# Third group's queries and keys as 32 by 32 tiles, its masks and exponentials inside the first output product, state sums of 40 columns behind the first group

## The chip, the cores and the metric

One of the eight cores of a Trainium2 chip runs the kernel. Its engines work side by side: TensorE (PE) multiplies matrices into PSUM, VectorE (DVE), ScalarE (ACT) and GpSimd (POOL) work on tiles, and the SP queue issues most DMAs. The metric is the time of one execution on the device in microseconds, the median of several.

## The reference

Two blocks follow each other. The first is an mLSTM cell on 4 batches of 8 heads (32 batch-heads), 768 steps, head dimension 40. Each step updates a state of 40 by 40 and a vector of 40 per head, with exponential gates that are kept stable by a running maximum m:

```python
m_new = np.maximum(f_gate[:, :, t] + m, i_gate[:, :, t])
f_stab = np.exp(f_gate[:, :, t] + m - m_new)
i_stab = np.exp(i_gate[:, :, t] - m_new)
C = f_stab[:, :, None, None] * C + i_stab[:, :, None, None] * np.einsum('bhd,bhe->bhde', vt, kt)
n = f_stab[:, :, None] * n + i_stab[:, :, None] * kt
h_tilde = np.einsum('bhde,bhe->bhd', C, qt)
denom = np.maximum(np.abs(nq), 1.0)          # nq = n . q
y[:, :, t] = o * h_tilde / denom             # o = sigmoid(o_gate)
```

The second takes the result as 3072 tokens of 320 features through a SwiGLU block with 1536 hidden features: `(silu(x @ w_gate) * (x @ w_val)) @ w_out`. The activations are float32; the three weight matrices arrive as float64 and are converted on the chip.

## The kernel before, in words

The 768 steps are cut into six groups of 128 steps (n = 0 to 5), each of two halves of 64. For a group, the cell works in a chunked form. Scores are the products of keys and queries (`scores`, L327). Weights come from the gates: `weights_load` fetches the running maxima to `w_sb`, `weights_sub` (L441) subtracts, `weights_mask` (L446) sets what lies in the future to a very small number on GpSimd, `weights_exp` (L450) takes exponentials on ScalarE. `weigh` (L334) multiplies scores by weights. `weigh_values` (L337) makes the weighted values `vw_sb`, `add` (L348) sums keys times weighted values for the state, and `next_state` decays the state on GpSimd (L357) and adds the sum on VectorE (L359). `attend` makes the parts from the state (L367) and from within the half (L372), `gather`, `gate` and `divide` finish the cell's output. Heads come in pairs, and pairs in two parts, P = 0 and 1.

`scores` and `attend` need keys and queries with features on partitions (`kT`, `qT`). There are two ways to get there. `turn` transposes on TensorE: loads of whole rows go to `k_sb` and `q_sb`, 32 transposes for each P (L292) go to PSUM, and eight copies (L117, L119) for the two P bring them to SBUF. `turn_squares` (L317) lets VectorE transpose blocks of 32 by 32 in SBUF, and wants its input loaded as such blocks: `load_squares` (L311) issues 16 small DMAs for each tensor, into a tile of zeros, as 40 features leave 24 of 64 rows empty. Groups 1 and 2 use `turn`, groups 3 to 5 use `turn_squares`. `q_sq` is a view of `q_sb`; the tile `k_sq` is allocated after the first output product, with a memset (L748). `k_sb` keeps plain keys for `add`.

The second block of group g runs beside the cell of group n = g + 1. `hidden(g, m)`, for twelve blocks m, multiplies by gate and value weights (L634, 20 products into two PSUM banks), ScalarE applies Silu (L639) and VectorE the product (L640). The output product of group 0 is `project_all` (L657): four banks, one per batch, summed over m in step. Later groups use `project` (L650), a batch at a time. `result` copies a bank to `z_sb` (two buffers, L644) and sends it. PSUM has two rings of four banks, "gen" for L634, L650 and L657, and "cell" for the attention. In group 0 the weights are converted as well: `convert` scales on ScalarE (L186, L188), joins on VectorE (L195, L196) and rounds on GpSimd or VectorE (L203).

Nothing is planned by a scheduler. The order of each engine's instructions is the order in which the program writes them; semaphores then hold each until its inputs are there. `slots` (L706 for group 0, L754 for later ones) and `after` (L725) list what is written behind block m of `hidden` and of `project_all`. Behind `project_all` before the change stand, in this order, the four output copies (in `result`), the third group's two exponentials, its two sigmoids (`sig`, L453) and its weighted values (L737 to L742). The transposes of group 2 are in slots 0 and 1 of g = 1.

Of the kernel before, what the change touches and what calls it, by code (L numbers as in the profile page):

```python
# [9 lines left out]
F32 = mybir.dt.float32  # L10
# [4 lines left out]
ALU = mybir.AluOpType  # L15
# [3 lines left out]
L = 128  # L19
SUB = 64  # L20
# [4 lines left out]
def kernel(  # L25
# [18 lines left out]
    nc = tc.nc  # L44
    B, H, S, D = q.shape
# [4 lines left out]
    PP = BH // 2  # L50
    DP = 64
# [5 lines left out]
    NKC = DM // HP  # L57
# [13 lines left out]
    conv = early_scope.enter_context(tc.tile_pool(name="conv", bufs=2))  # L71
# [4 lines left out]
    def bank(name, tag="cell"):  # L76
        return psum.tile([128, 512], F32, name=name, tag=tag)

    def half(i):
        return slice(i * SUB, (i + 1) * SUB)  # L80

    def heads(P):
        return slice(P * UH, (P + 1) * UH)

    k_sb = const.tile([128, BH, DP], F32)
    q_sb = const.tile([128, BH, DP], F32)
    v_sb = const.tile([128, BH, D1], F32)
    o_sb = const.tile([128, BH, D], F32)
    w_sb = const.tile([128, BH, SUB], F32)
    vw_sb = const.tile([128, BH, D1], F32)  # L90
    kT = const.tile([128, PP, L], F32)
    qT = const.tile([128, PP, L], F32)
# [150 lines left out]
    for u in range(B):  # L243
        r = slice(u * BH, (u + 1) * BH)
# [58 lines left out]
    SQ = 32  # L303

    def load_squares(dst, a, c):
        for two in range(2):
            for s in range(2):
                r = slice((2 * two + s) * SQ, (2 * two + s + 1) * SQ)
                w = min(SQ, D - s * SQ)
                for t in range(L // SQ):  # L310
                    nc.sync.dma_start(out=dst[r, :, t, 0:w],  # L311
                                      in_=a[:, two:H:2, ds(c * L + t * SQ, SQ), ds(s * SQ, w)].rearrange("b h p d -> p (b h) d"))

    def turn_squares(src, dst):
        for P in range(2):
            a = slice(P * UA, (P + 1) * UA)
            nc.vector.transpose(out=dst[:, a].rearrange("p a t -> p (a t)"), in_=src[:, a].rearrange("p a t d -> p (a t d)"))  # L317

    q_sq = q_sb.rearrange("p (a x) d -> p a (x d)", x=2).rearrange("p a (t d) -> p a t d", d=SQ)
# [16 lines left out]
    def weigh_values(eng, P):  # L336
        eng.tensor_tensor(vw_sb[:, heads(P)], v_sb[:, heads(P)], w_sb[:, heads(P), last].to_broadcast([128, UH, D1]),  # L337
                          op=ALU.mult)

    def small(name, n=UA):  # L340
        return bank(name)[:, 0:n * D1].rearrange("p (a d) -> p a d", d=D1)

    def add(P):
        ps = [small("add") for _ in range(2)]
        for a in range(UA):
            for i, two in QUAD:
                h = P * UH + 2 * a + two
                nc.tensor.matmul(ps[i][half(two), a, :], lhsT=k_sb[half(i), h, :], rhs=vw_sb[half(i), h, :],  # L348
                                 start=True, stop=True)
        return ps  # L350

    def state(s):
        return C_ring[s % 3]

    def next_state(s, P, ps):
        a = slice(P * UA, (P + 1) * UA)
        nc.gpsimd.tensor_tensor(state(s + 1)[:, a], state(s)[:, a],  # L357
                                dec[:, s - 2, a].unsqueeze(2).to_broadcast([128, UA, D1]), op=ALU.mult)
        nc.vector.tensor_tensor(state(s + 1)[:, a], state(s + 1)[:, a], ps, op=ALU.add)  # L359


    def attend(n, P):
# [86 lines left out]
    def weights_exp(P):  # L449
        nc.scalar.activation(w_sb[:, heads(P)], w_sb[:, heads(P)], AF.Exp)  # L450

    def sig(P):
        nc.scalar.activation(o_sb[:, heads(P)], o_sb[:, heads(P)], AF.Sigmoid)  # L453
# [7 lines left out]
    def rows(u):  # L461
        return slice(u * BH, (u + 1) * BH)

    A, V, G = nc.scalar, nc.vector, nc.gpsimd
# [188 lines left out]
    def project_all(g, after):  # L653
        ps = [bank("o_ps", "gen")[:, 0:DM] for _ in range(B)]
        for m in range(NFC):
            for u in range(B):
                nc.tensor.matmul(ps[u], lhsT=hid(g, m)[:, ts(u, L)], rhs=wo_sb[:, m, :], start=(m == 0),  # L657
                                 stop=(m == NFC - 1))
            for f in after.get(m, ()):
                f()  # L660
        for u in range(B):
            result(g, u, ps[u])

    live = {}
# [5 lines left out]
    def do_weigh(P):  # L670
        weigh(P, live.pop(("sp", P)))

    def do_add():
        for P in range(2):
            live["add", P] = add(P)

    def do_state(s, P):
        for i, ps in enumerate(live.pop(("add", P))):
# [16 lines left out]
    def load_all(dst, a, n):  # L695
# [3 lines left out]
    run = lambda f, *a: (lambda: f(*a))  # L699
# [6 lines left out]
    slots = {  # L706
        0: [run(first_state, 1, A), run(load_all, k_sb, k, 1), run(load_all, q_sb, q, 1)],
        1: [run(late_maxima), run(piece_load, 6, h_sb[:, NH - NKC:])],
        2: [run(weights_load, 1), run(load_all, v_sb, v, 1), run(decay_rows)],
        3: [run(late_turns)],  # L710
        4: [run(decay)],
        5: [run(turn, 0, (A, A), (A, V))],
        6: [run(turn, 1, (A, A), (A, V)), run(piece_load, 7)],
        7: [run(weights_sub, 1, 0), run(weights_sub, 1, 1), run(weights_mask, 0), run(weights_mask, 1)],
        8: [run(weights_exp, 0), run(weights_exp, 1), run(weigh_values, G, 0), run(weigh_values, G, 1),
            run(piece_load, 8)],
        9: [run(do_scores), run(do_weigh, 0), run(do_weigh, 1), run(load_all, o_sb, o_gate, 1)],
        10: [run(do_add), run(do_state, 2, 0), run(do_state, 2, 1)],
        11: [run(do_attend, 1, 0), run(do_gather, 1, 0, False), run(piece_load, 9)],
    }  # L720
    for m in range(NFC):
        hidden(0, m, [run(convert, j, V if j in on_vector else None) for j in ahead[m]])
        for f in slots.get(m, ()):
            f()
    after = {  # L725
        0: [run(do_attend, 1, 1), run(convert, 14), run(sig, 0), run(sig, 1), run(do_gate, 0)],
        1: [run(do_gather, 1, 1), run(weights_load, 2), run(load_all, v_sb, v, 2)],
        2: [run(do_divide, 1, 0), run(convert, 15)],
        3: [run(do_divide, 1, 1), run(load_all, k_sb, k, 2), run(load_all, q_sb, q, 2), run(load_all, o_sb, o_gate, 2)],
        4: [run(convert, 16), run(seam, 1, 0, (A, V, A, V))],  # L730
        5: [run(seam, 1, 1, (A, V, A, V))],
        6: [run(convert, 17)],
        8: [run(weights_sub, 2, 0), run(weights_mask, 0)],
        9: [run(weights_sub, 2, 1), run(weights_mask, 1)],
    }
    project_all(0, after)
    weights_exp(0)  # L737
    weights_exp(1)
    sig(0)
    sig(1)  # L740
    weigh_values(G, 0)
    weigh_values(G, 1)  # L742
    early_scope.close()
    late = ctx.enter_context(tc.tile_pool(name="late", bufs=1))
    xTs.append(late.tile([128, NKC, TW], F32, name="xT1"))
# [1 line left out]
    k_sq = late.tile([128, PP, L // SQ, SQ], F32, name="k_sq")  # L747
# [4 lines left out]
    for g in range(1, NG):  # L752
        n, f = g + 1, g + 2
        slots = {m: [] for m in range(NFC)}  # L754
        if n < NG:
            slots[0] = [run(turn, 0, (A, V), (A, V))] if n == 2 else [run(turn_squares, q_sq, qT)]
            slots[1] = [run(turn, 1, (A, V), (A, V))] if n == 2 else [run(turn_squares, k_sq, kT)]
            if n == 2:
                slots[1].append(run(nc.gpsimd.memset, q_sb, 0.0))
            slots[3] = [run(do_scores), run(do_weigh, 0)]  # L760
            slots[4] = [run(do_weigh, 1)]
            slots[5] = [run(do_add), run(do_state, 2 * n, 0)]
            slots[6] = [run(do_state, 2 * n, 1)]
            slots[7] = [run(do_attend, n, 0), run(do_gather, n, 0)]
            slots[8] = [run(do_divide, n, 0), run(send_squares, 0)]
            slots[9] = [run(do_attend, n, 1), run(do_gather, n, 1)]
            slots[10] = [run(do_divide, n, 1), run(send_squares, 1)]
        if f < NG:
            slots[2] += [run(load_squares, q_sq, q, f), run(load_squares, k_sq, k, f)]
            slots[5].append(run(load_all, k_sb, k, f))  # L770
            slots[9] += [run(load_all, v_sb, v, f), run(weights_load, f)]
            slots[10].append(run(load_all, o_sb, o_gate, f))
        for m in range(NFC):
            hidden(g, m)
            for s in slots[m]:
                s()
        for u in range(B):
            if f < NG and u < 2:
                weights_sub(f, u)
                weights_mask(u)  # L780
            if f < NG and u == 2:
                weights_exp(0)
                weights_exp(1)
                sig(0)
                sig(1)
                weigh_values(nc.gpsimd, 0)
                weigh_values(nc.gpsimd, 1)
            if n < NG and u >= 2:
                turn_inputs(n, 2 * u - 4)
                turn_inputs(n, 2 * u - 3)  # L790
            project(g, u)
# [30 lines left out]
```

## Time and profile before

| | before |
|---|---|
| median of 3 runs | 568.58 us (565.74 to 569.22) |
| profiled execution | 567.32 us, its span 565.2 us |
| TensorE busy | 554.4 us, 98% |
| weight loads / VectorE / ScalarE / GpSimd busy | 57% / 40% / 25% / 18% |
| mean granted TensorE clock | 0.996 |
| DMA | 45.05 MB, mean 80 GB/s |

Times in the trace count from the span's start. Up to about 55 us the kernel loads its inputs and does the first group's attention; `hidden` of group 0 lasts to about 100 us, `project_all` to about 133 us, and each later group takes some 87 us. A row of the timeline has a start, a length, the engine, the line, the operation, its output and input tiles, and in brackets the idle time of the engine before it with what ended that. In the chain of work that ended last, a row has a start, a length, the engine and the line.

### The profile page before, as it was taken

Reading aid. Unit: us, or ns where it says so; the run is one execution under the profiler, and the core shown is the slowest. Engines: PE = TensorE matmul, PEld = TensorE weight load, DVE = VectorE, ACT = ScalarE, POOL = GpSimd, SP = SyncE. Lnnn points to the kernel's source line nnn. Section 1 sums busy time; section 2 is a strip of 40 time slices with the busy share of each in tenths; the row PEclk is TensorE's granted clock in tenths of the full one; section 3 lists DMA queues with packets and bytes.
Section 4 is the critical chain, followed back from the end, with each engine's and each line's share of the span. In section 5 each row is a group of like instructions: output and inputs, shape, how many; then the busy total and the mean of one; then the engine's idle time right before and its main releaser. Section 6 shows DMA issues by size and latency. Waiting matters only on the chain.

```text
span 565.2 us, 11653 instructions
## 1 busy us (share of the span) xinstructions
PE 554.4 (98%) x5055; PEld 322.7 (57%) x5056; DVE 225.4 (40%) x379; ACT 139.3 (25%) x208; POOL 103.8 (18%) x95
## 2 busy tenths in 40 slices
PE   8997999999999999999999999999999999999997
PEld 4855545665555476455566455567455557544475
DVE  5775576880334531434612424613432631011100
ACT  4365446435401015110104201104211010111100
POOL 2132344555211123002105001206001100000000
PEclk9999999999999999999999999999999999999999
DMA  9999991594362395353295253196000131000000
GB/s 124 182 271 187 179 264 22 151 152 95 41 79 26 50 148 110 44 53 49 38 149 111 41 66 49 31 145 110 24 2 2 26 59 46 12 1 1 1 23 24
DMA packets 211227, 45.05 MB, mean 80 GB/s; under 512 B 201736, under 2 KB 206344, under 8 KB 211176
## 3 DMA queue, kind: packets, MB, share of 16 engines
q1 hardware_dynamic: 208596, 40.14, 44.5%
q10 hardware_dynamic: 2580, 4.16, 3.3%
q8 instruction: 40, 0.66, 0.5%
q14 instruction: 11, 0.09, 0.1%
HBM read 35.03 MB, written 4.01 MB: 69 GB/s over the span
## 4 chain that ended last, share of the span: by engine, by line
PE 84%; DMA 5%; SPq 4%; DVE 3%; ACT 2%; POOL 1%; issue 1%; ACTq 0%; DVEq 0%; POOLq 0%
PE gv_ps L634 49%; PE o_ps L650 23%; PE o_ps L657 5%; SPq L113 3%; DMA raw<-in_moe_w_val_dram 3%; DMA h_sb<-in_moe_w_gate_dram 2%; PE intra L372 2%; PE inter L367 2%; PE sp L327 1%; PE add L348 1%; DVE wgv_sb L196 1%; DVE wgv_sb L195 1%; POOL C L357 1%; PE tp_kq L292 0%; SPq L161 0%
## 5 line engine op out<-in xcount | busy, mean ns | idle before, releaser
L634 PE MATMUL gv_ps<-xT,wgv_sb 64*128 64x512 f32 x1440 | 320.7, 596 | 4.5 <-POOL wgv_sb L203 3.6
L634 PEld LDWEIGHTS gv_ps<-xT,wgv_sb 64*128 64x128 f32 x1440 | 144.5, 188 | 158.9 <-issue 149.4
L640 DVE TENSOR_TENSOR h_sb<-sg,gv_ps 128x512 f32<-128x512 f32 x72 | 49.4, 687 | 227.7 <-ACT sg L639 227.7
L650 PE MATMUL o_ps<-wo_sb,h_sb 128*128 128x320 f32 x480 | 130.5, 433 | 0.0
L650 PEld LDWEIGHTS o_ps<-wo_sb,h_sb 128*128 128x128 f32 x480 | 90.8, 190 | 41.0 <-issue 3.8
L639 ACT ACTIVATE sg<-gv_ps 128x512 f32<-128x512 f32 x72 | 43.0, 597 | 261.3 <-PE gv_ps L634 261.3
L357 POOL TENSOR_TENSOR C<-C,dec 128x328 f32<-128x328 f32 x20 | 14.5, 737 | 146.6 <-DVE C L359 146.6
L446 POOL TENSOR_SCALAR_AFFINE_SELECT w_sb<-w_sb 64x1024 f32<-64x1024 f32 x20 | 28.2, 1409 | 58.9 <-DVE w_sb L441 58.0
L644 ACT COPY z_sb<-o_ps 128x320 f32<-128x320 f32 x24 | 10.2, 424 | 101.8 <-PE o_ps L650 90.7
L657 PE MATMUL o_ps<-wo_sb,h_sb 128*128 128x320 f32 x96 | 26.9, 437 | 0.0
L393 POOL TENSOR_TENSOR o_sb<-o_sb,y_sb 128x640 f32<-128x640 f32 x10 | 14.2, 1425 | 61.7 <-DVE y_sb L384 61.7
L441 DVE TENSOR_TENSOR w_sb<-g_T,w_sb 128x1024 f32<-128x1024 f32 x10 | 13.1, 1354 | 26.8 <-DMA w_sb<-M_dram 26.8
L657 PEld LDWEIGHTS o_ps<-wo_sb,h_sb 128*128 128x128 f32 x96 | 17.9, 190 | 7.2
L416 DVE STREAM_TRANSPOSE xT<-x_sq 128x640 f32<-128x640 f32 x16 | 12.5, 821 | 23.5 <-DMA x_sq<-x_sb 23.5
L384 DVE TENSOR_TENSOR y_sb<-y_sb,intra 64x328 f32<-64x328 f32 x40 | 19.7, 493 | 0.7
L203 POOL TENSOR_TENSOR wgv_sb<-wgv_sb,low 128x640 int32<-128x640 int32 x8 | 13.3, 1667 | 29.2 <-DVE wgv_sb L196 29.2
L337 POOL TENSOR_TENSOR vw_sb<-v_sb,w_sb 128x656 f32<-128x656 f32 x10 | 13.0, 1318 | 8.6 <-issue 6.4
L367 PEld LDWEIGHTS inter<-C,qT 64*64 64x64 f32 x640 | 10.2, 134 | 7.3 <-issue 6.1
L359 DVE TENSOR_TENSOR C<-C,add 128x328 f32<-128x328 f32 x20 | 9.9, 493 | 10.5 <-POOL C L357 10.5
L203 POOL TENSOR_TENSOR wo_sb<-wo_sb,low 128x640 int32<-128x640 int32 x6 | 10.2, 1706 | 15.0 <-DVE wo_sb L196 10.5
L334 DVE TENSOR_TENSOR w_sb<-sp,w_sb 128x512 f32<-128x512 f32 x20 | 12.7, 682 | 0.2 <-issue 0.2
L372 PE MATMUL intra<-v_sb,w_sb 64*64 64x41 f32 x640 | 12.3, 228 | 0.4 <-DVE C L359 0.3
(127 smaller groups left out, 353.1 us busy)
## 6 DMA issues: line engine op xcount, KB each, us to landing
w_sb<-M_dram SPq DMA_DIRECT2D x10, 512.0 KB, 6.8
x_sq<-x_sb SPq DMA_DIRECT2D x128, 40.0 KB, 2.0
k_sb<-in_k_dram SPq DMA_DIRECT2D x12, 320.0 KB, 5.9
v_sb<-in_v_dram SPq DMA_DIRECT2D x12, 320.0 KB, 7.0
o_sb<-in_o_gate_dram SPq DMA_DIRECT2D x12, 320.0 KB, 5.6
raw<-in_moe_w_out_dram SPq DMA_DIRECT2D x3, 1280.0 KB, 7.8
out_dram<-z_sb SPq DMA_DIRECT2D x24, 160.0 KB, 1.8
q_sb<-in_q_dram SPq DMA_DIRECT2D x6, 320.0 KB, 8.7
```

Of the source, the lines that this page charges most:

```text
L113: nc.sync.dma_start(out=dst[:, heads(P), 0:D], in_=tokens(a, c, P))
L203: (eng or nc.gpsimd).tensor_tensor(dst, dst, lo, op=ALU.add)
L357: nc.gpsimd.tensor_tensor(state(s + 1)[:, a], state(s)[:, a], dec[:, s - 2, a].unsqueeze(2).to_broadcast([128, UA, D1]), op=ALU.mult)
L367: nc.tensor.matmul(inter[two][half(i), a, :], lhsT=qT[half(two), P * UA + a, half(i)], rhs=state(2 * n + i)[half(two), P * UA + a, :], sta ...
L372: nc.tensor.matmul(intra[i][half(c), a, :], lhsT=w_sb[half(i), h, :], rhs=v_sb[half(i), h, :], start=True, stop=True)
L384: nc.vector.tensor_tensor(t, t, intra[i][half(c)], op=ALU.add)
L446: nc.gpsimd.affine_select(w, w, compare_op=ALU.is_ge, fill=NEG, base=0, pattern=[[0, UH], [1, SUB]], channel_multiplier=-1)
L634: nc.tensor.matmul(ps[i], lhsT=wgv_sb[half(i), m, PAIRS[kc][i] if g < 2 else kc, :], rhs=x[half(i), kc, :], start=(kc == 0), stop=(kc == N ...
L639: nc.scalar.activation(sg, ps[0], AF.Silu)
L640: nc.vector.tensor_tensor(hid(g, m), sg, ps[1], op=ALU.mult)
L650: nc.tensor.matmul(p, lhsT=hid(g, m)[:, ts(u, L)], rhs=wo_sb[:, m, :], start=(m == 0), stop=(m == NFC - 1))
L657: nc.tensor.matmul(ps[u], lhsT=hid(g, m)[:, ts(u, L)], rhs=wo_sb[:, m, :], start=(m == 0), stop=(m == NFC - 1))
```

## The change

Four things change.

- The third group's queries and keys (n = 2) come as 32 by 32 tiles. `q_sb` is set to zero in slot 7 of group 0 and its tiles are loaded in slot 10. The key tiles get a buffer of the conversion pool (`early_squares`), set to zero and loaded behind block 3 of `project_all`. VectorE transposes queries behind block 8 and keys behind block 11. The transposes on TensorE in slots 0 and 1 of g = 1 go, as do the plain loads of queries; the plain keys are loaded behind block 7.
- The third group's subtractions and masks are written behind blocks 5 and 7 in place of 8 and 9, and conversion 17 behind block 5 in place of 6.
- Its exponentials, sigmoids and weighted values are written behind blocks 9 and 10 of `project_all`, and so ahead of the four output copies.
- `add` takes 40 columns of the keys in place of 64 for every group but the second (n = 1). What it writes is then 40 rows in each half of the partitions, and `next_state` adds in two instructions of 40 rows each.

```diff
--- before.py
+++ after.py
@@ -78,6 +78,10 @@
 
     def half(i):
         return slice(i * SUB, (i + 1) * SUB)
+
+
+    def feats(i):
+        return slice(i * SUB, i * SUB + D)
 
     def heads(P):
         return slice(P * UH, (P + 1) * UH)
@@ -340,12 +344,13 @@
     def small(name, n=UA):
         return bank(name)[:, 0:n * D1].rearrange("p (a d) -> p a d", d=D1)
 
-    def add(P):
+    def add(n, P):
         ps = [small("add") for _ in range(2)]
+        rows, w = (half, DP) if n == 1 else (feats, D)
         for a in range(UA):
             for i, two in QUAD:
                 h = P * UH + 2 * a + two
-                nc.tensor.matmul(ps[i][half(two), a, :], lhsT=k_sb[half(i), h, :], rhs=vw_sb[half(i), h, :],
+                nc.tensor.matmul(ps[i][rows(two), a, :], lhsT=k_sb[half(i), h, 0:w], rhs=vw_sb[half(i), h, :],
                                  start=True, stop=True)
         return ps
 
@@ -356,7 +361,9 @@
         a = slice(P * UA, (P + 1) * UA)
         nc.gpsimd.tensor_tensor(state(s + 1)[:, a], state(s)[:, a],
                                 dec[:, s - 2, a].unsqueeze(2).to_broadcast([128, UA, D1]), op=ALU.mult)
-        nc.vector.tensor_tensor(state(s + 1)[:, a], state(s + 1)[:, a], ps, op=ALU.add)
+        for r in (slice(0, 128),) if s < 4 else (feats(0), feats(1)):
+            c = state(s + 1)[r, a]
+            nc.vector.tensor_tensor(c, c, ps[r], op=ALU.add)
 
 
     def attend(n, P):
@@ -670,9 +677,9 @@
     def do_weigh(P):
         weigh(P, live.pop(("sp", P)))
 
-    def do_add():
+    def do_add(n):
         for P in range(2):
-            live["add", P] = add(P)
+            live["add", P] = add(n, P)
 
     def do_state(s, P):
         for i, ps in enumerate(live.pop(("add", P))):
@@ -711,35 +718,40 @@
         4: [run(decay)],
         5: [run(turn, 0, (A, A), (A, V))],
         6: [run(turn, 1, (A, A), (A, V)), run(piece_load, 7)],
-        7: [run(weights_sub, 1, 0), run(weights_sub, 1, 1), run(weights_mask, 0), run(weights_mask, 1)],
+        7: [run(weights_sub, 1, 0), run(weights_sub, 1, 1), run(weights_mask, 0), run(weights_mask, 1),
+            run(nc.gpsimd.memset, q_sb, 0.0)],
         8: [run(weights_exp, 0), run(weights_exp, 1), run(weigh_values, G, 0), run(weigh_values, G, 1),
             run(piece_load, 8)],
         9: [run(do_scores), run(do_weigh, 0), run(do_weigh, 1), run(load_all, o_sb, o_gate, 1)],
-        10: [run(do_add), run(do_state, 2, 0), run(do_state, 2, 1)],
+        10: [run(do_add, 1), run(do_state, 2, 0), run(do_state, 2, 1), run(load_squares, q_sq, q, 2)],
         11: [run(do_attend, 1, 0), run(do_gather, 1, 0, False), run(piece_load, 9)],
     }
     for m in range(NFC):
         hidden(0, m, [run(convert, j, V if j in on_vector else None) for j in ahead[m]])
         for f in slots.get(m, ()):
             f()
+    def early_squares(part):
+        if part == 0:
+            live["k_sq"] = conv.tile([128, 4 * NKC * 128], F32, name="raw")[:, 0:PP * L].rearrange("p (a t d) -> p a t d", a=PP, d=SQ)
+            nc.gpsimd.memset(live["k_sq"], 0.0)
+            load_squares(live["k_sq"], k, 2)
+        else:
+            turn_squares(live.pop("k_sq"), kT)
+
     after = {
         0: [run(do_attend, 1, 1), run(convert, 14), run(sig, 0), run(sig, 1), run(do_gate, 0)],
         1: [run(do_gather, 1, 1), run(weights_load, 2), run(load_all, v_sb, v, 2)],
         2: [run(do_divide, 1, 0), run(convert, 15)],
-        3: [run(do_divide, 1, 1), run(load_all, k_sb, k, 2), run(load_all, q_sb, q, 2), run(load_all, o_sb, o_gate, 2)],
+        3: [run(do_divide, 1, 1), run(load_all, o_sb, o_gate, 2), run(early_squares, 0)],
         4: [run(convert, 16), run(seam, 1, 0, (A, V, A, V))],
-        5: [run(seam, 1, 1, (A, V, A, V))],
-        6: [run(convert, 17)],
-        8: [run(weights_sub, 2, 0), run(weights_mask, 0)],
-        9: [run(weights_sub, 2, 1), run(weights_mask, 1)],
+        5: [run(seam, 1, 1, (A, V, A, V)), run(convert, 17), run(weights_sub, 2, 0), run(weights_mask, 0)],
+        7: [run(weights_sub, 2, 1), run(weights_mask, 1), run(load_all, k_sb, k, 2)],
+        8: [run(turn_squares, q_sq, qT)],
+        9: [run(weights_exp, 0), run(weights_exp, 1), run(weigh_values, G, 0), run(weigh_values, G, 1)],
+        10: [run(sig, 0), run(sig, 1)],
+        11: [run(early_squares, 1)],
     }
     project_all(0, after)
-    weights_exp(0)
-    weights_exp(1)
-    sig(0)
-    sig(1)
-    weigh_values(G, 0)
-    weigh_values(G, 1)
     early_scope.close()
     late = ctx.enter_context(tc.tile_pool(name="late", bufs=1))
     xTs.append(late.tile([128, NKC, TW], F32, name="xT1"))
@@ -753,13 +765,12 @@
         n, f = g + 1, g + 2
         slots = {m: [] for m in range(NFC)}
         if n < NG:
-            slots[0] = [run(turn, 0, (A, V), (A, V))] if n == 2 else [run(turn_squares, q_sq, qT)]
-            slots[1] = [run(turn, 1, (A, V), (A, V))] if n == 2 else [run(turn_squares, k_sq, kT)]
-            if n == 2:
-                slots[1].append(run(nc.gpsimd.memset, q_sb, 0.0))
+            if n > 2:
+                slots[0] = [run(turn_squares, q_sq, qT)]
+                slots[1] = [run(turn_squares, k_sq, kT)]
             slots[3] = [run(do_scores), run(do_weigh, 0)]
             slots[4] = [run(do_weigh, 1)]
-            slots[5] = [run(do_add), run(do_state, 2 * n, 0)]
+            slots[5] = [run(do_add, n), run(do_state, 2 * n, 0)]
             slots[6] = [run(do_state, 2 * n, 1)]
             slots[7] = [run(do_attend, n, 0), run(do_gather, n, 0)]
             slots[8] = [run(do_divide, n, 0), run(send_squares, 0)]
```

## The prediction

> **What bounds the kernel now.** I read the page's first table, a row of the groups by line (the 32 by 32 transposes, for their price), then the chain that ended last, then the timeline of the one stretch where the chain leaves TensorE after 103 us.
>
> ```profile
> PE 554.4 (98%) x5055; PEld 322.7 (57%) x5056; DVE 225.4 (40%) x379; ACT 139.3 (25%) x208; POOL 103.8 (18%) x95
> ...
> L317 DVE STREAM_TRANSPOSE qT<-q_sb 128x1024 f32<-128x1024 f32 x6 | 7.1, 1219 | 0.0
> ```
>
> TensorE is the bound. Only its own work taken away, or a hole in it closed, shortens the kernel. The chain in order of time, from the end of the first group's output product (L657) to the third group's scores (L327):
>
> ```profile
> 120.57 12.05 PE o_ps L657 x44
> ...
> 135.48 1.28 ACT L450
> ...
> 136.78 2.01 ACT w_sb L450 x2
> ...
> 138.80 1.28 ACT L453
> ...
> 140.10 1.36 ACT o_sb L453 x2
> ...
> 141.48 1.28 ACT L639
> ...
> 142.77 0.61 ACT sg L639
> ...
> 154.69 2.02 PE sp L327 x128
> 156.71 8.79 PE gv_ps L634 x40
> 165.50 2.01 PE add L348 x128
> ...
> 224.03 17.37 PE gv_ps L634 x80
> 241.40 2.02 PE sp L327 x128
> ```
>
> The reader should see ScalarE's exponentials (L450), sigmoids (L453) and three table loads ahead of the Silu of the group's first block. TensorE restarts at 133.62 and needs 154.69 - 133.62 = 21.07 us to the scores. A later group needs 17.37 us for the same four blocks. The difference, 3.70 us, is the transposes of L292 (64, about 2 us by the chain's 0.99 us per 32) and the wait for that late Silu. The timeline just before:
>
> ```profile
> 118.87 1.54 POOL L203 TENSOR_TENSOR wo_sb<-wo_sb,low 128x640 int32<-128x640 int32 x1 [0.85 <-DVE wo_sb L196]
> ...
> 123.23 3.70 DVE L441 TENSOR_TENSOR w_sb<-g_T,w_sb 128x1024 f32<-128x1024 f32 x2
> 123.46 2.39 POOL L203 TENSOR_TENSOR wo_sb<-wo_sb,low 128x640 int32<-128x640 int32 x1 [3.05 <-DVE wo_sb L196]
> ...
> 125.80 5.76 POOL L446 TENSOR_SCALAR_AFFINE_SELECT w_sb<-w_sb 64x1024 f32<-64x1024 f32 x4
> 132.11 0.96 ACT L644 COPY z_sb<-o_ps 128x320 f32<-128x320 f32 x2 [9.49 <-PE o_ps L657]
> ...
> 133.62 4.56 PE L634 MATMUL gv_ps<-xT,wgv_sb 64*128 64x512 f32 x20
> ```
>
> GpSimd masks until 131.56. ScalarE then copies two output banks (L644), which lets TensorE start the next group with no gap.
>
> **What the Trainium skill says.** "TensorE: Matmul & The Clock Gate", section "Architectural detail", calls ScalarE and VectorE strict first-in first-out; the trace agrees (the Silu at 142.77 stands behind six instructions it doesn't need). Its section "LDWEIGHTS" prices a weight load by its columns at 1/1.2 ns each, rows free. The trace agrees: 128 `add` products of 64 columns, four array tiles at once, take 2.01 us, 63 ns a round; 128 `sp` products that stream 64 columns, not 41, take 2.02 us, so the load sets the pace. The same page's "Part 1" has a clock gate that looks at 3.41 us windows. Here the granted clock was 0.66 over 55 to 60 us, after a hole from about 51.6 to 55.2; a wait of 1.30 us at 88.2 left it at 1.00. "SBUF — State Buffer", section "SBUF: two separate sides", says GpSimd and VectorE lock each other out of a shared port pair for a whole instruction. The trace agrees: the first mask took 2.13 us while L441 ran, the other three 1.14.
>
> **The change part by part.**
>
> *Transposes leave TensorE.* The 64 transposes (L292) and their eight copies go: with the late Silu, 3.70 us at most. In place: 32 small DMAs, two memsets, four VectorE transposes. Query tiles: the memset (1.80 us, row of the later one) comes behind the masks that end at 86.66 and ahead of the value products (L337), which began at 88.55, so 0 to 0.3 us, taken 0. SP idles from 83.24 to 97.25; 16 issues at 8.57 us fit (88.5 to 97.1), and the last output-weight piece, queued behind them, still goes at about 97.3. Key tiles: memset 1.81 us from 118.02, in POOL's gaps of 0.85 and 3.05 us ahead of the two roundings; the first slips by 1 us, the second not. SP then issues 16 tiles (9.07 us) from about 120 to 129, plain keys (4.03 us) to 133, and only then the output rows, which are not ready before 135.8. If each cover failed, the memsets would cost 1.8 us each at most. The four transposes, 4 x 1.22 = 4.9 us, lie in VectorE's idle 126.9 to 143.4 and have to end by 141.
>
> *Masks.* They move in the program from slots 8 and 9 to 5 and 7, but their predecessors on VectorE and POOL stay the same: conversion 17, its rounding, L441. In the trace nothing but these held them. So I keep their end at 131.56 and save nothing.
>
> *Exponentials and sigmoids.* They now stand ahead of the four output copies on ScalarE. The exp table loads early (0, hidden in the wait for masks). The second exponential starts when the masks end: 131.60 + 1.05 = 132.65; sigmoid table 1.28, so 133.95; two sigmoids 1.36, so 135.35; two copies 0.85 to 0.96, so 136.25. Queued behind the waiting exponential are those copies, and TensorE waits for them, since all four banks of its ring hold the outputs. It restarts at 136.25 in place of 133.62: a new stall of 2.63 us. Output copies three and four need the first output DMA (1.84 us), are done by 139, and are wanted at 140.6. The Silu is no longer late. So scores begin at 136.25 + 17.37 = 153.62, against 154.69: 1.07 us won of the 3.70.
>
> *State sums.* 40 columns in place of 64, in four groups. By the rows above, 64 columns cost 63 ns a round; 24 columns fewer at 0.83 ns would save 20 ns x 32 rounds x 4 groups = 2.6 us at most. The floor that the page gives, in "Back-to-back issue gap", about 25 ns for small products, counts twice for f32 (an estimate: 40 products of 512 columns take 8.78 us, two tiles at once, so 439 ns or two passes at the page's price), leaving about 60 ns and 0.4 us. No saving is the lower end; a loss is excluded, as instructions and array positions stay the same. I take the middle, 1.4 us. The split of the sums into two halves of 40 rows adds 16 VectorE sums of 0.49 us, 7.9 us. They hide: in the fourth group the last sum ended at 261.8, and TensorE wanted its banks at 263.9, so 0.98 us more fits. Without cover it would be 1 us a group.
>
> *Sum.* 1.07 + 1.4 = 2.5 us less. The profiled execution took 567.32 us (span 565.2 and 2.1 around it): 564.8. It lies 1.26 under the median of 568.58, so on the median's level I say 566.1.
>
> **Rivals.**
>
> (1) *The clock drops, and ScalarE is held longer.* Place: POOL ahead of the masks. If the key memset's 1.81 us isn't absorbed, the masks end at 133.4, TensorE restarts at 138.1, and a hole of 4.6 us holds a whole window of the gate; at 55 us such a hole cost half of 3.41 us, 1.7. Price 1.8 + 1.7 against 2.5: 1.0 slower, 569.6. It decides from a restart about 0.8 us later than mine, if the clock drops; with the drop alone 567.8. For it: the second rounding runs right ahead of the masks. Against: POOL's gaps of 3.9 us.
>
> (2) *The exponentials come in time.* Were the masks 3.5 us earlier, all 3.70 + 1.4 = 5.1 would be won, 563.5 (562.3 with the full column saving). For it: that the slots come earlier. Against: L441 began at 123.23 directly behind conversion 17, with no DMA wait shown.
>
> (3) *Key tiles land late.* VectorE's Silu product would stand behind the transposes, and TensorE's third block behind that. With SP's slowest 16 issues of any kind (13.06 us) and the worst landing for queries (8.7 us) they are there at 141.8, about when they hurt; double that latency gives some 5 us, 571.
>
> (4) *40 columns do nothing:* 567.5.
>
> **How the numbers follow.** Forecast, with (4) at its edge: 0.47, 566.1, own range 564.9 to 567.5. Rival 1: 0.30, of which about half is the clock alone. Rival 2: 0.11. Rival 3: 0.07. Something not named: 0.05. The three runs of before spread by 3.5 us, which widens the ends: 562.8 to 570.5. One per cent, about what a measurement of this kernel can tell from no change, is 562.9 and 574.3. Faster by more: most of rival 2's better half, 0.08. Slower by more: 0.09 for rival 3 at its worst and what I haven't seen. Within: 0.83.
>
> **What the new profile would show.** ScalarE's second exponential at about 131.6 and the first output copy behind the sigmoids at about 135.4; TensorE idle from 133.5 to about 136.2, the only new hole; no transposes in the third group; 80 hidden products in 17.4 us up to the scores; `add` rounds of 43 to 63 ns; the granted clock after 136 at 1.00, or 0.5 for 3.4 us if rival 1 holds. I am wrong if the masks end before 129, if TensorE waits elsewhere in the second group, or if `add` takes longer than 2.01 us.

## The result, and the profile after

| | before | changed |
|---|---|---|
| median of 20 runs each | 567.94 us (565.03 to 571.52) | 563.92 us (560.99 to 569.57) |
| ratio, 95% interval | 1 | 0.9925 (0.9905 to 0.9945) |
| TensorE busy in the profiled execution | 554.4 us | 552.9 us |

The changed kernel is faster by 0.75%, some 4 us. Its one profiled execution took 569.57 us (span 567.7 us) and is the slowest of the 20: the second group's scores already came 3.4 us late (89.22 us against 85.85), before anything that the change touches, and TensorE's clock was halved three times. So its total isn't to be set against 567.32 us, but stretches inside it can be read.

The lines named here have numbers 4 to 7 higher in the changed kernel: scores are L331 (L327 before), gate and value products L641 (L634), the first output product L664 (L657), exponentials L457 (L450), sigmoids L460 (L453), Silu L646 (L639), output copies L651 (L644), their DMAs L652 (L645), `add` L353 (L348). From the page of the changed kernel, the busy times and one new group (the state sums of 40 rows):

```profile
PE 552.9 (97%) x4992; PEld 319.4 (56%) x4992; DVE 235.7 (42%) x395; ACT 137.3 (24%) x204; POOL 105.8 (19%) x96
...
L366 DVE TENSOR_TENSOR C<-C,add 40x328 f32<-40x328 f32 (+1 forms) x36 | 17.7, 492 | 11.3 <-POOL C L362 11.0
```

TensorE has 63 recorded products fewer (the 64 transposes; a record can be missing), VectorE 10 us more work. The chain that ended last, from the third group's masks to the fourth group's scores (start, length, engine and line):

```profile
133.79 1.15 POOL w_sb L453
134.97 1.06 ACT w_sb L457
136.04 1.28 ACT L460
137.34 1.36 ACT o_sb L460 x2
138.70 0.32 ACT z_sb L651
139.06 19.46 PE gv_ps L641 x80
158.52 2.02 PE sp L331 x128
160.54 8.78 PE gv_ps L641 x40
169.33 1.56 PE add L353 x120
...
227.58 17.37 PE gv_ps L641 x80
244.95 2.02 PE sp L331 x128
```

The transposes are gone, and the 80 products of `hidden` stand in one piece up to the scores. `add` takes 1.56 us in place of 2.01. What is new is at the top: masks, the second exponential, a table load, the sigmoids and one output copy now lie on the chain, ahead of TensorE's restart. The timeline around it:

```profile
129.18 5.75 POOL L453 TENSOR_SCALAR_AFFINE_SELECT w_sb<-w_sb 64x1024 f32<-64x1024 f32 x4
...
134.97 1.06 ACT L457 ACTIVATE w_sb<-w_sb 128x1024 f32<-128x1024 f32 x1 [1.36 <-POOL w_sb L453]
...
137.34 1.36 ACT L460 ACTIVATE o_sb<-o_sb 128x640 f32<-128x640 f32 x2
...
138.61 0.73 ACT L651 COPY z_sb<-o_ps 128x320 f32<-128x320 f32 x2
139.04 3.19 SPq L652 DMA_DIRECT2D out_dram<-z_sb  x4
...
139.06 7.44 PE L641 MATMUL gv_ps<-xT,wgv_sb 64*128 64x512 f32 x24 [1.97 <-ACT z_sb L651]
```

TensorE stands for 1.97 us until the first copy (L651) frees a bank. Why 19.46 us for 80 products that take 17.37 a group later is seen in the windows of the same stretch (stretch, length, then busy time of PE, PEld, DVE, ACT and POOL, the granted clock, DMA share, GB/s):

```profile
137.00:140.00 3.00, 1.03 (x5) 0.76 (x6) 0.74 (x1) 2.33 (x5) 2.78 (x3) 1.00 1.05 97
140.00:144.00 4.00, 4.00 (x14) 2.56 (x12) 0.00 (x0) 2.13 (x3) 0.30 (x1) 0.57 0.56 172
144.00:148.00 4.00, 4.00 (x21) 2.65 (x19) 0.69 (x1) 0.60 (x1) 0.00 (x0) 1.00 0.69 73
```

The clock was halved from 140.48 to 143.89, behind the hole; that cost half of 3.41 us, 1.7.

Two measures compare all runs below, each inside one trace. The *seam* is the time from the start of the last product of group 0's output (`project_all`) to the first product of the third group's scores, so it holds the transposes, the hole and the wait for the Silu: 21.36 us before (133.26 to 154.62), 21.79 here (136.66 to 158.45), so 20.1 without the halved clock. The *pitch* is the time from one group's scores to the next group's, the mean of the three such times from the third group to the sixth. Each holds one `add`: 86.71 us before, 86.38 here. The fourth `add` of 40 columns, in the sixth group, lies behind the last scores; it is counted with the same gain, as it is as short as the others in the chain of e1 (1.53 us).

### The profile page after: what moved, and what is told of

It is laid out like the page before. It is cut to its first block, busy times and chain, and to the rows that moved or that the text cites. A ratio compares the mean times of both kernels' runs of the same rounds, so it can differ in the third digit from the quotient of the medians.

```text
span 567.7 us, 11598 instructions
## 1 busy us (share of the span) xinstructions
PE 552.9 (97%) x4992; PEld 319.4 (56%) x4992; DVE 235.7 (42%) x395; ACT 137.3 (24%) x204; POOL 105.8 (19%) x96
## 4 chain that ended last, share of the span: by engine, by line
PE 79%; DMA 7%; DVE 4%; SPq 4%; POOL 2%; ACT 2%; issue 1%; POOLq 0%; ACTq 0%; DVEq 0%
PE gv_ps L641 50%; PE o_ps L657 23%; SPq L117 3%; DMA h_sb<-in_moe_w_val_dram 2%; DMA raw<-in_moe_w_gate_dram 2%; DMA o_sb<-in_o_gate_dram 2%; PE inter L374 2%; PE intra L379 1%; PE sp L331 1%; SPq L315 1%; PE add L353 1%; DVE y_sb L391 1%; POOL wo_sb L207 1%; POOL C L362 1%; ACT w_sb L457 0%
## 5 line engine op out<-in xcount | busy, mean ns | idle before, releaser
L641 PE MATMUL gv_ps<-xT,wgv_sb 64*128 64x512 f32 x1440 | 323.2, 600 | 8.8 <-POOL wgv_sb L207 3.4
L641 PEld LDWEIGHTS gv_ps<-xT,wgv_sb 64*128 64x128 f32 x1440 | 145.1, 189 | 166.7 <-issue 149.9
L657 PE MATMUL o_ps<-wo_sb,h_sb 128*128 128x320 f32 x480 | 130.5, 433 | 0.0
L657 PEld LDWEIGHTS o_ps<-wo_sb,h_sb 128*128 128x128 f32 x480 | 90.8, 190 | 41.0 <-issue 3.8
L646 ACT ACTIVATE sg<-gv_ps 128x512 f32<-128x512 f32 x72 | 43.0, 597 | 265.5 <-PE gv_ps L641 265.5
L453 POOL TENSOR_SCALAR_AFFINE_SELECT w_sb<-w_sb 64x1024 f32<-64x1024 f32 x20 | 28.4, 1422 | 58.3 <-DVE w_sb L448 57.4
L651 ACT COPY z_sb<-o_ps 128x320 f32<-128x320 f32 x24 | 10.1, 423 | 92.8 <-PE o_ps L657 91.1
L664 PE MATMUL o_ps<-wo_sb,h_sb 128*128 128x320 f32 x96 | 26.9, 437 | 0.0
L366 DVE TENSOR_TENSOR C<-C,add 40x328 f32<-40x328 f32 (+1 forms) x36 | 17.7, 492 | 11.3 <-POOL C L362 11.0
L664 PEld LDWEIGHTS o_ps<-wo_sb,h_sb 128*128 128x128 f32 x96 | 17.9, 190 | 7.2
L199 DVE TENSOR_SCALAR wgv_sb<-top 128x640 uint32<-128x640 uint32 x12 | 8.3, 695 | 12.4 <-ACT top L190 12.4
```

What stands on the lines that cost most here:

```text
L366: nc.vector.tensor_tensor(c, c, ps[r], op=ALU.add)
L453: nc.gpsimd.affine_select(w, w, compare_op=ALU.is_ge, fill=NEG, base=0, pattern=[[0, UH], [1, SUB]], channel_multiplier=-1)
L641: nc.tensor.matmul(ps[i], lhsT=wgv_sb[half(i), m, PAIRS[kc][i] if g < 2 else kc, :], rhs=x[half(i), kc, :], start=(kc == 0), stop=(kc == N ...
L646: nc.scalar.activation(sg, ps[0], AF.Silu)
L657: nc.tensor.matmul(p, lhsT=hid(g, m)[:, ts(u, L)], rhs=wo_sb[:, m, :], start=(m == 0), stop=(m == NFC - 1))
```

## The experiments

**The change again (e1), and with 64 columns (e2).** The same kernel, and the same with the state sums as before:

```diff
-        rows, w = (half, DP) if n == 1 else (feats, D)
+        rows, w = half, DP
...
-        for r in (slice(0, 128),) if s < 4 else (feats(0), feats(1)):
+        for r in (slice(0, 128),):
```

> The changed kernel once more, for a second profile. Theory A (the gain is the part between the two halves of the trace that I can name: the start of the second group, and the 40 columns): 2.7 us under the kernel before where the clock stays whole behind the hole at the end of the first output product, 1.0 under it where it halves for 3.4 us. Theory B (something else gains too, in the loading stage or in how often the clock halves): 4 us under it, as the medians of 20 runs say, and the profile has the first block after loading earlier than the 31.8 us and 55.2 us of before, or a granted clock with fewer drops than before.

> The change without its 40 columns: the state sums take 64 columns again in all groups, and the new state is added in one instruction. Theory A: 1.4 us more than the change, from four groups of 0.36 us, and 128 of these products start over 1.85 us, as before, in place of 1.40 to 1.55. Rival (the columns do nothing for the total, as the 0.4 us are lost again at the next wait): no difference.

Measured: e1 564.82 us against 567.26, ratio 0.9952 (0.9928 to 0.9977). e2 566.21 us, ratio 0.9993 (0.9968 to 1.0019). The timeline of e1:

```profile
139.65 1.36 ACT L460 ACTIVATE o_sb<-o_sb 128x640 f32<-128x640 f32 x2
140.92 0.73 ACT L651 COPY z_sb<-o_ps 128x320 f32<-128x320 f32 x2
...
141.38 17.76 PE L641 MATMUL gv_ps<-xT,wgv_sb 64*128 64x512 f32 x80 [1.98 <-ACT z_sb L651]
```

From its chain, the scores of the third and the fourth group and the `add` behind them:

```profile
159.13 2.02 PE sp L331 x128
...
245.36 2.02 PE sp L331 x128
...
256.17 1.56 PE add L353 x118
```

The same hole of 1.98 us, and no halved clock behind it: 80 products in 17.76 us. The seam is 20.10 us, 1.26 less than before. In e2 the seam is the same (20.12) and the pitch is the old one (86.75, against 86.25 in e1). So the two parts of the gain lie in different places and add up: the seam gives 1.26 us, the columns 0.46 us in each of four groups, 1.8. The sum is 3.1 us; e1's ratio is 2.7 us (1.3 to 4.1). So e1 came as its first account said, and e2's median lies 1.4 us above e1's, as expected of it. The first 20 runs gave more: their ratio is 4.3 us (3.1 to 5.4), with the sum at the edge. What they had beyond it isn't found in a trace.

**The columns alone (e5).** The kernel before, with 40 columns and the split sums and nothing else:

```diff
+        rows, w = (half, DP) if n == 1 else (feats, D)
...
-                nc.tensor.matmul(ps[i][half(two), a, :], lhsT=k_sb[half(i), h, :], rhs=vw_sb[half(i), h, :],
+                nc.tensor.matmul(ps[i][rows(two), a, :], lhsT=k_sb[half(i), h, 0:w], rhs=vw_sb[half(i), h, :],
...
-        nc.vector.tensor_tensor(state(s + 1)[:, a], state(s + 1)[:, a], ps, op=ALU.add)
+        for r in (slice(0, 128),) if s < 4 else (feats(0), feats(1)):
...
```

> The kernel before with the 40 columns alone (and the new state added in two halves of 40 rows). Theory A: groups from scores to scores take 86.3 in place of 86.71 us, four of them count, so 1.6 us less than before; nothing else moves, as the longer additions on VectorE stay hidden. Rival (the additions are not hidden without the tiles, or the columns only help beside them): no gain, or a wait of TensorE ahead of the products with the state.

Measured: 565.56 us against 567.70, ratio 0.9961 (0.9945 to 0.9977), 2.2 us less. Seam 21.36 as before, pitch 86.23: 4 x 0.48 = 1.9 us. The groups by form, first the kernel before, then e5 (busy us, mean ns of one, idle before):

```profile
L348 PE MATMUL add<-vw_sb,k_sb 64*64 64x41 f32 x640 | 10.4, 228 | 0.0
L348 PEld LDWEIGHTS add<-vw_sb,k_sb 64*64 64x64 f32 x640 | 9.8, 135 | 3.8 <-issue 3.0 <-DVE w_sb L334 0.8
```

```profile
L352 PE MATMUL add<-vw_sb,k_sb 64*40 64x41 f32 x512 | 6.4, 201 | 0.0
L352 PEld LDWEIGHTS add<-vw_sb,k_sb 64*40 64x40 f32 x512 | 5.9, 115 | 3.0 <-issue 3.0
```

A load of 40 columns takes 20 ns less than one of 64. That difference is 24 columns at the price that the Trainium skill states ("TensorE: Matmul & The Clock Gate", section "LDWEIGHTS": 1/1.2 ns a column); the whole load takes longer than the price, 115 ns. Of the 20 ns a round of four products keeps 14 to 15 (0.46 to 0.48 us over 32 rounds). The split sums on VectorE cost nothing that shows: `intra` waits for the state once, 0.3 us, before and after alike.

**Exponentials back behind the output copies (e6).** Tiles and 40 columns stay. Only exponentials, sigmoids and weighted values go back to where they were:

```diff
-        9: [run(weights_exp, 0), run(weights_exp, 1), run(weigh_values, G, 0), run(weigh_values, G, 1)],
-        10: [run(sig, 0), run(sig, 1)],
...
     project_all(0, after)
+    weights_exp(0)
+    weights_exp(1)
+    sig(0)
+    sig(1)
+    weigh_values(G, 0)
+    weigh_values(G, 1)
```

> The change with exponentials, sigmoids and weighted values behind the output copies, as in the kernel before; tiles and 40 columns stay. Theory A: no hole at the end of the first output product; the Silu of the second group's first block comes at about 142.8 us on the clock of the profile before, TensorE waits some 1.7 us ahead of the third block, and from the last product of the first output to the scores it takes 19.4 us (before 21.4, change 20.1). So 0.7 us less than the change: the move of the exponentials lost what it was to win. Rival (the move is what gains): 2 us or more above the change, near the kernel before.

Measured: 566.83 us, ratio 0.9992 (0.9969 to 1.0015). My theory failed; the rival, which has it slower than the change by 2 us, was right (e1's median is 2.0 us lower). The seam is 22.26 us, longer than before the change though 64 transposes are gone. The timeline of e6:

```profile
129.90 1.85 SPq L117 DMA_DIRECT2D k_sb<-in_k_dram  x2
131.80 0.96 ACT L651 COPY z_sb<-o_ps 128x320 f32<-128x320 f32 x2 [9.49 <-PE o_ps L664]
132.25 5.96 SPq L652 DMA_DIRECT2D out_dram<-z_sb  x4
...
136.95 0.80 ACT L651 COPY z_sb<-o_ps 128x320 f32<-128x320 f32 x2 [4.19 <-DMA out_dram<-z_sb]
...
145.05 1.09 ACT L646 ACTIVATE sg<-gv_ps 128x512 f32<-128x512 f32 x2
...
145.70 9.57 PE L641 MATMUL gv_ps<-xT,wgv_sb 64*128 64x512 f32 x40 [3.34 <-ACT sg L646]
```

TensorE restarts with no hole, but the third copy waits 4.19 us for the first output row to leave `z_sb`. Before the change it was 1.41:

```profile
134.48 0.98 ACT L644 COPY z_sb<-o_ps 128x320 f32<-128x320 f32 x2 [1.41 <-DMA out_dram<-z_sb]
```

Behind the copies on ScalarE stand the exponentials, the sigmoids and the Silu, and TensorE then waits 3.34 us for that Silu. The two loads of plain keys (320 KB each) stand just ahead of the output rows on SP: the first row's issue took 1.49 us (0.38 is the median of the four), and in the chain it is 4.60 us from issue to arrival. In the chain of e5, where no loads stand there, the second row takes 1.84 us. The two rows, e6's first:

```profile
132.25 4.60 DMA out_dram<-z_sb
```

```profile
135.24 1.84 DMA out_dram<-z_sb
```

**Plain keys later (e9).** To show that cause: e6, with the loads of plain keys behind the output rows.

```diff
-        7: [run(weights_sub, 2, 1), run(weights_mask, 1), run(load_all, k_sb, k, 2)],
+        7: [run(weights_sub, 2, 1), run(weights_mask, 1)],
...
+            if n == 2:
+                slots[0] = [run(load_all, k_sb, k, 2)]
```

> The kernel with exponentials and sigmoids behind the output copies, and with the third group's two loads of plain keys moved from behind block 7 of the first output product to behind the first block of the second group, so behind the output rows on SP. Theory C (the plain keys, queued on SP just ahead of the output rows, delay the rows' landing, so ScalarE's third copy waits 4.2 us in place of 1.4, and the Silu with it): the wait falls to under 2 us, TensorE's wait ahead of the third block from 3.3 to about 1 us, from the last product of the first output to the scores 19.4 to 20.0 us in place of 22.3; 2 to 2.5 us less than with the plain keys ahead. Rival (the 16 key tiles themselves, or the value products, hold the rows): the wait stays at about 4 us and the time as it was.

Measured: 563.78 us against 567.37, ratio 0.9934 (0.9914 to 0.9954). The timeline of e9:

```profile
134.18 3.25 SPq L652 DMA_DIRECT2D out_dram<-z_sb  x4
...
136.11 0.96 ACT L651 COPY z_sb<-o_ps 128x320 f32<-128x320 f32 x2 [1.42 <-DMA out_dram<-z_sb]
...
137.48 1.76 SPq L117 DMA_DIRECT2D k_sb<-in_k_dram  x2
...
145.03 9.57 PE L641 MATMUL gv_ps<-xT,wgv_sb 64*128 64x512 f32 x40 [0.94 <-ACT sg L646]
```

The third copy's wait is back at 1.42 us, TensorE's wait for the Silu falls from 3.34 to 0.94, and the seam to 19.66. The plain keys ahead of the rows were the cause; the 16 key tiles, the rival, stand there in both. In its chain a row takes 1.82 us from issue to arrival, 2.8 less than the 4.60 of e6. Of these, 1.1 lie in the issue (1.49 against some 0.35); how the rest came about, in the queue or in the transfers themselves, isn't separated. This run also gives the tiles' own worth with the ScalarE order of before: 21.36 - 19.66 = 1.70 us.

**The sigmoids, behind or first (e3, e4, e8).** Of the path that now holds TensorE, 2.64 us are the sigmoids with their table. e3 moves them behind the output copies, e4 and e8 (the same kernel twice) ahead of the exponentials, behind block 6, where ScalarE is waiting for the masks anyway:

```diff
+        6: [run(sig, 0), run(sig, 1)],
...
-        10: [run(sig, 0), run(sig, 1)],
```

(This is the edit of e4 and e8. e3 has the same line removed and `sig(0)`, `sig(1)` behind `project_all` in its place.)

> The change with the two sigmoids moved behind the four output copies; the exponentials stay ahead of them. Theory A (ScalarE's queue holds the copies, and the copies hold TensorE): the copies start 2.7 us earlier, right behind the second exponential, the hole of some 2.1 us closes to under 0.5 us, no halved clock behind it; 2 us less than the change, and 1.7 more in those executions in which the clock halved. Rival (TensorE's restart is held by something else, a bank or the tiles): no difference to the change.

> The change with the two sigmoids moved ahead of the exponentials, into the time in which ScalarE waits for the masks. Theory A: the same hole closed, so within 0.5 us of the kernel with the sigmoids behind the copies. Rival: the output gates land too late (after about 128 us), the sigmoids hold the exponentials, and the restart is as late as in the change or later.

> The kernel with the sigmoids ahead of the exponentials once more, for a second profile and a narrower interval. Theory A: from the last product of the first output to the scores 17.8 us (before 21.4), four groups of 86.3 us; 5.2 us less than before. Rival (its first result was a matter of the loading stage): 2.5 us less, as the change.

Measured: e3 563.18 us, ratio 0.9942 (0.9923 to 0.996). e4 562.95 us, 0.9916 (0.9885 to 0.9946), and e8 562.18 us, 0.9892 (0.9865 to 0.992). The timeline of e4:

```profile
127.08 0.73 ACT L460 ACTIVATE o_sb<-o_sb 128x640 f32<-128x640 f32 x1
...
128.21 0.74 ACT L460 ACTIVATE o_sb<-o_sb 128x640 f32<-128x640 f32 x1 [0.40 <-DMA o_sb<-in_o_gate_dram]
129.10 1.28 ACT L457 ACT_TABLE_LOAD   x1
...
136.17 1.06 ACT L457 ACTIVATE w_sb<-w_sb 128x1024 f32<-128x1024 f32 x1 [1.36 <-POOL w_sb L453]
...
137.13 0.73 ACT L651 COPY z_sb<-o_ps 128x320 f32<-128x320 f32 x2
...
138.20 17.55 PE L641 MATMUL gv_ps<-xT,wgv_sb 64*128 64x512 f32 x80
...
155.68 0.52 PE L331 MATMUL sp<-qT,kT 64*64 64x64 f32 x20
```

The sigmoids now lie in ScalarE's wait for the masks. Their table load is gone: nothing but copies and conversions has run since the second group's sigmoids loaded it (109.39 us), and the trace has five table loads for L460 in place of six. The first copy comes at 137.13, ahead of the last product's start at 137.84, and TensorE goes on without a hole: seam 17.84 us (17.80 in e8), some 0.4 over the 17.37 us of a later group. Against the change that is 2.3 us less, the hole of 2.0 us and a little more. In e3 the hole is closed too, but the Silu then stands behind the sigmoids:

```profile
137.98 0.78 ACT L651 COPY z_sb<-o_ps 128x320 f32<-128x320 f32 x2 [4.25 <-DMA out_dram<-z_sb]
...
140.07 1.36 ACT L460 ACTIVATE o_sb<-o_sb 128x640 f32<-128x640 f32 x2
...
142.75 1.08 ACT L646 ACTIVATE sg<-gv_ps 128x512 f32<-128x512 f32 x2
```

Its third copy waits 4.25 us, with the plain keys ahead of the rows as in e6; the seam is 19.18 us, 0.9 under the change and not 2 as expected. In e4 a like wait (3.89 us) harms nothing, as nothing but the Silu stands behind it. So the expectation that e4 would come within 0.5 us of e3 failed: by the seam it is 1.3 us better.

**The hole filled (e7).** Nine products on zeros (128 x 512) behind the first output product, so that TensorE's clock sees no hole:

```diff
     project_all(0, after)
+    burn(9)
```

> The change with nine added products on a tile of zeros behind the first output product (about 2 us of TensorE work that nobody reads), so that TensorE works through the hole while it waits for the output copies. Theory A, with the clock: the restart comes at the same time, within 0.2 us; no halved clock in the 5 us behind it, and the mean loss of granted clock per execution falls from 3.4 us of the change to about that of the kernel before, 2.9. Rival (the clock's drops come from the loading stage alone): loss and time as in the change.

Measured: 564.99 us, ratio 0.9952 (0.9935 to 0.9969), the seam 20.10 us as in e1 and no halved clock behind the hole. As e1 shows none either, this doesn't tell what the hole costs in clock. Over the runs, the mean loss (span times one minus the granted clock) is 3.38 us in e1, 3.38 in e7, and 2.84 and 2.98 in the runs of before beside them. That the loss would fall to 2.9 with the filler didn't come true. The 20 runs of the result lost only 2.67 us, so no loss is shown that belongs to the change; this stays open.

**The masks' new place** has no run of its own. Made alone in the kernel before, this move leaves the order of the instructions on every engine as it was, so it can win nothing by itself. In the change, masks back in slots 8 and 9 would let the query transposes of slot 8 go ahead of the second subtraction on VectorE; what that costs isn't shown.

The runs side by side. The worked-out difference, in us, is that of the seam plus four times that of the pitch, against 21.36 and 86.71:

| | seam | pitch | worked out | measured (95%) |
|---|---|---|---|---|
| e1 the change | 20.10 | 86.25 | -3.1 | -2.7 (-4.1 to -1.3) |
| e2 64 columns | 20.12 | 86.75 | -1.1 | -0.4 (-1.8 to +1.1) |
| e3 sigmoids behind | 19.18 | 86.30 | -3.8 | -3.3 (-4.4 to -2.3) |
| e4 sigmoids first | 17.84 | 86.28 | -5.2 | -4.8 (-6.5 to -3.1) |
| e8 the same | 17.80 | 86.33 | -5.1 | -6.1 (-7.7 to -4.5) |
| e5 columns alone | 21.36 | 86.23 | -1.9 | -2.2 (-3.1 to -1.3) |
| e6 exponentials behind | 22.26 | 86.27 | -0.9 | -0.5 (-1.8 to +0.9) |
| e7 hole filled | 20.10 | 86.25 | -3.1 | -2.7 (-3.7 to -1.8) |
| e9 plain keys later | 19.66 | 86.21 | -3.7 | -3.7 (-4.9 to -2.6) |

(Measured: the ratio and its ends less one, times the median of before beside them.) Each worked-out number lies in its interval, so two places of the trace are enough to account for all nine. The intervals are 1.8 to 3.4 us wide; they wouldn't show another part of less than a microsecond.

## Why the prediction was right

The forecast was 2.5 us less; the first 20 runs gave 4.0 by their medians, e1 2.4, and the traces 3.1. The sign was right, and the mechanism in the main. The median of 563.92 us lies in the whole range of 562.8 to 570.5, but below the forecast's own range of 564.9 to 567.5. That 2.5 came so near is in part luck, as errors of opposite sign met in it. By its steps:

- *Transposes leave TensorE, 3.70 us at most with the late Silu.* Right. Of the excess over a later group (21.0 us from restart to scores, against 17.4), e9 shows 1.7 us for the transposes; the rest is the Silu. In the change the same count is 17.69 us (e1), so nearly all of it was won.
- *The masks keep their end.* Right. The second exponential was forecast at 131.60 and began at 134.97 in an execution that ran 3.40 us later (its last output product started at 136.66, before at 133.26): 131.57.
- *A new stall of 2.63 us.* Right in place, too large. The path was forecast item by item (exponential, table, sigmoids) and came so. But I took two output copies to be wanted, and TensorE restarted 0.04 us behind the first one. The restart came 2.04 us later than with no hole (139.06 against 133.62 + 3.40), 0.6 less than forecast. Against that, the 80 products behind it took 17.69 us and not 17.37. So 1.26 us was won at the seam, not 1.07.
- *State sums, 0.4 to 2.6 us, taken 1.4.* Mis-sized: 1.8 by the pitch, 2.2 by e5's ratio. The 1.4 was the middle of two ends and no working. In e1 the 128 products took 1.53 to 1.56 us in place of 2.01, so 48 to 49 ns a round of four in place of 63. My floor of 60 ns doesn't follow from the terms that it was built on: twice 25 ns is 50, and a floor of 50 would leave 13 ns a round, 1.7 us in all, near the 1.8 that came. Whether a floor lies there isn't shown, as no run has fewer than 40 columns. That the load sets the pace was more than equal times for 41 and 64 streamed columns could show; e5 bears it out for 14 to 15 of 20 ns.
- *Covers cost nothing.* Right for the change: from the second group's scores to the last output product it takes 47.44 us (89.22 to 136.66), before 47.41 (85.85 to 133.26), so memsets, tile loads, VectorE's transposes and split sums all hide. But the reason given for SP, that plain keys end at 133 ahead of the output rows, holds only because the change makes those rows late. With the rows at their old time (e6) the plain keys cost 22.26 - 19.66 = 2.60 us. My expectation of e6, which left the SP queue out, failed on that.
- *Rival 1, the clock.* It can happen: once in the two profiles of the change, behind a hole of 1.97 us and not 4.6. (Nor need a hole of 4.6 us hold a whole window of 3.41: that takes a window that begins in its first 1.2 us.) The wait of 1.30 us at 88.2 that I set against it was the weight loads'; the products stood still for only 0.48 us there, so it told little. ScalarE wasn't held longer, as POOL's gaps took the memset. *Rival 2*, exponentials in time, is what e4 and e8 make of it, by moving the sigmoids and not the masks. *Rival 3*, late key tiles, wasn't seen: the scores follow the hidden products with no wait.

So the change is worth 3.1 us by two parts that don't touch: 1.26 at the seam (the exponentials' move 22.26 - 20.10 = 2.16 won, less 0.90 that tiles with the plain keys ahead would have cost alone), and 1.8 from the columns. A version with the sigmoids ahead of the exponentials beats both kernels: 562.2 to 563.0 us, about 1% under the kernel before.

## What to carry to other kernels

When work moves ahead of something that frees a buffer, add up the path of the engine that does both, from the last input to the first release: here 1.06 + 1.28 + 1.36 + 0.32 us, of which only the exponential depended on the late masks. The sigmoids could be put into the wait ahead of it, where their table was still loaded. When loads move earlier, look at which stores stand behind them on the same queue, and which buffers these stores release. A part that repeats in every group is measured best by its pitch inside one trace, where loading times and medians don't enter.

## What the runs showed of the hardware

- A small DMA issued behind large ones can arrive much later: an output row (160 KB) behind two key loads (320 KB each) on SP took 4.60 us to arrive in e6, 1.82 us in e9 with the keys behind it.
- A hole of 2 us in TensorE's work can be followed by a halved clock or not. In the profiled execution of the change the drops began at 34.66, 58.56 and 140.48 us and lasted 3.413 us each; the distances are 7 and 24 times that length, so they lie on a fixed grid. The hole (137.09 to 139.06) lay whole in the window before the third, and left TensorE idle for 58% of it. In e1 and e2 the hole was as long, but it was split between two windows of their grids (from their first drops at 34.97 and 35.49), of which none was idle for more than 41% and 47%, and no drop followed. The Trainium skill ("TensorE: Matmul & The Clock Gate", "Part 1") speaks of free-running windows of this length, but of an idle window; here a good half of one was enough. The idle share alone doesn't decide: in e6 a window with 55% idle (140.84 to 144.25) had no drop, while in the loading stage of e7 one with 40% idle (51.09 to 54.50) had one behind it. What else counts stays open.
- Four products at once on array tiles of 64 x 40 take 48 to 49 ns a round, with weight loads of 115 ns each (63 ns and 135 ns for 64 columns), below the 60 ns that the prediction took as the least.
